# Two weights of a slot converted as one 1024-column tile, splits between the layers on VectorE, and the second block three slots behind the first

## The chip, the cores and the metric

The kernel runs on one core of a Trainium2 chip. The metric is the device time of one execution in microseconds (us). Before the change three runs gave 947.40, 947.91 and 949.22 us, with a median of 947.91 us.

## The reference, cut to what matters

Four sequences of 576 tokens go through windowed attention with eight heads of 64 columns (heads 0 to 3 look back 32 positions, heads 4 to 7 look back 128 positions in steps of four). The result, 2304 tokens by 512 columns, goes through two MLPs of 2048 hidden columns; the first has a leaky ReLU, the second a softplus.

```python
scores = np.where(masks, scale * q @ k.T, -1e9)        # per batch and head
attn = np.exp(scores - scores.max(-1)); attn /= attn.sum(-1) + 1e-9
x = concat_heads(attn @ v)                             # 2304 x 512
h = x @ w_in;  x = np.maximum(0.01 * h, h) @ w_out     # first layer
h = x @ w_in2; out = softplus(h) @ w_out2              # second layer
```

The weights arrive as 64-bit floats, q, k and v as 32-bit floats. On the chip each weight is turned from two 32-bit words into one 32-bit float, and that float is split into a high part in TensorE's fast format (fp32r) and a low part, the rest. Every product of an MLP is three matmuls: high by high, high by low, low by high.

## The kernel before, in words

**Slots.** The hidden columns of a layer are cut into 16 groups f of 128. A slot is one group f for one block of tokens. It has a first product (12 matmuls, `first_product`, L622, tile h) and, two slots later on TensorE (LAG = 2), a second product (12 matmuls, `g2`, L665, tile yp). Between them ScalarE applies the leaky ReLU (`g1_leaky`, L638, tile hc) and rounds to the high part (`g1_hi`, L643, gh), and VectorE subtracts to get the low part (`g1_lo`, L647, gl). There are two banks for h, two tiles hc, three gh and three gl. The second layer has the same shape (h in L622, softplus in L718 to L738, gh L744, gl L748, second product yo in L761).

**Blocks.** The first layer goes over eight blocks of tokens: 256, 256, 352 and five of 288. The list `order` sets the slots. Block 0 runs LEAD = 6 slots alone, then blocks 1 and 0 alternate, (1,0), (0,6), (1,1), (0,7) and so on, until both have all 16 groups; the later blocks run one after the other.

**Conversion of a weight.** A piece is one weight (w_in or w_out) of one group f, 512 columns wide. Its raw words are loaded on SyncE's DMA queue (L224, L228, tile raw, 512 KB). ScalarE does rebias (L234, tile cf) and low (L248), VectorE shift (L239, tile cp), join (L243) and add (L252). In the first layer ScalarE then writes the high part (`split_hi`, L272) and VectorE the low part (`split_lo`, L277) into the weight tile w. The pieces of the second layer are converted during the first layer and stored to DRAM (L261); in the last 16 slots of the first layer each is loaded again into the place of a used weight (`reload`, L266), split by ScalarE (L272) and by GpSimd (L277 on POOL). The reload of w_in waits for the last first product that reads its place, that of w_out for the last second product.

**Attention.** A pair is two heads on a window of 288 tokens; there are 8 windows w of 4 pairs. Windows 0 and 1 are early: k and q rows are loaded (L389), transposed by TensorE (L431, tile tr), and the scores (L480, L484, tile sc) are copied out, one half by ScalarE and one by VectorE (`scores_copy`, L498 and L500). GpSimd takes the maximum (`rowmax`, L535), VectorE subtracts it (L539), ScalarE takes the exponent (L542), TensorE multiplies with v (`pv`, L555), VectorE normalises (L565 to L567, tile xn), TensorE transposes back (`xT`, L575), and x is split (x_hi L596, x_lo L600). Block 0 needs window 0, block 1 also window 1, block 2 also window 2. The early tiles lie where weights of groups 6 to 15 come later.

**Order.** Nothing is ordered by hand. Every operation is an `Op` with an engine, a cost, what it depends on, buffers that it takes and gives back, and a target time; `run_schedule` plays the program with these costs and picks on each engine the ready Op with the earliest due time. The list that comes out is the program order on every engine, and an engine that meets an instruction whose data isn't there waits, with all that is queued behind it.

Of the kernel before, what the change touches and what calls it, by code (L numbers as in the profile page):

```python
# [22 lines left out]
def kernel(  # L23
# [62 lines left out]
    class Op:  # L86
        def __init__(self, eng, cost, fn, *args, deps=(), order=(), acq=(), rel=(),
                     target=None, margin=0.0, start=0.0, lib=None):
# [6 lines left out]
            self.lib = lib  # L95
# [3 lines left out]
    def run_schedule(slots):  # L99
# [13 lines left out]
        def lag(a, b):  # L113
            if b.eng == "bw":
                return 2.0
            return late.get(a.eng, LATS if a.eng == b.eng else LAT)
# [9 lines left out]
        for o in reversed(order):  # L126
# [4 lines left out]
            o.prio = o.raw - o.margin  # L131
# [21 lines left out]
        now = 0.0  # L153
        finish = []
        while True:
# [7 lines left out]
            for e in engines:  # L163
# [3 lines left out]
                for o in pools[e]:  # L167
                    if ready_at[o] <= now + 1e-9 and all(free[a] >= o.acq.count(a) for a in o.acq):
                        rank = o.prio + (HOLD if switch(o) else 0.0), o.n
# [8 lines left out]
                if e == "dve" and lib[0] == "standard":  # L178

                    best.end += 0.5 * min(best.cost, max(0.0, busy["pool"] - now))  # L180
# [29 lines left out]
    NRAW, NCV = 2, 3  # L210

    class Piece:
        def __init__(self, layer, f, which):
            self.layer, self.f, self.which = layer, f, which

        def load(self):
            src = wsrc[self.layer][self.which]
            f = self.f
            if self.layer == 0:
                raw = wpool.tile([P, 2 * DM], U32, tag=f"w{self.which}_{f}", name="raw")  # L220
            else:
                raw = wraw.tile([P, 2 * DM], U32, tag="raw", name="raw", bufs=NRAW)
            if self.which == 0:
# [5 lines left out]
            self.raw = raw.rearrange("p (n t) -> p n t", t=2)  # L229

        def rebias(self):
            self.cf = wraw.tile([P, DM], U32, tag="cf", name="cf", bufs=NCV)
# [4 lines left out]
        def shift(self):  # L237
            self.cp = wraw.tile([P, DM], U32, tag="cp", name="cp", bufs=1)
            nc.vector.tensor_single_scalar(  # L239
                out=self.cp, in_=self.cf, scalar=3, op=ALU.logical_shift_left)  # L240
# [10 lines left out]
        def add(self, eng):  # L251
            eng.tensor_tensor(out=self.cf, in0=self.cf, in1=self.raw[:, :, 0], op=ALU.add)  # L252

        def new_part(self):
            self.w = wpool.tile([P, 2, DM], F32R, tag=f"w{self.which}_{self.f}", name=f"w{self.which}")
            wparts[self.layer, self.f, self.which] = self.w
# [6 lines left out]
        def reload(self):  # L263
            self.new_part()
            self.cff = self.w[:, 1].bitcast(F32)
            nc.sync.dma_start(out=self.cff, in_=w2_d[self.f, self.which])  # L266

        def split_hi(self, eng):
            if self.layer == 0:
                self.new_part()  # L270
            if eng is nc.scalar:
                nc.scalar.activation(out=self.w[:, 0], in_=self.cff, func=AF.Copy)  # L272
            else:
                eng.tensor_copy(out=self.w[:, 0], in_=self.cff)

        def split_lo(self, eng):
            eng.tensor_sub(out=self.w[:, 1], in0=self.cff, in1=self.w[:, 0].bitcast(F32))  # L277
# [10 lines left out]
    NQB, NKB, NVB = 2, 2, 3  # L288
# [8 lines left out]
    early_kq = [wpool.tile([P, KT + T1], F32, tag=f"w0_{NF - NE + i}", name="ekq") for i in range(NE)]  # L297
    early_s = [wpool.tile([P, 2 * T1], F32, tag=t, name="es")
               for t in [f"w1_{NF - NE + i}" for i in range(NE)] + [f"w0_{NF - 2 * NE + i}" for i in range(NE)]]
    early_v = [wpool.tile([P, 2, DIL, D + 1], F32, tag=f"w1_{NF - 2 * NE + i}", name="ev") for i in range(NE)]  # L300
    early_mx = [wpool.tile([P, 2 * T1], F32, tag=f"w{i}_{NB}", name="emx") for i in range(2)]
# [49 lines left out]
    class Pair:  # L351
# [25 lines left out]
        def load_rows(self, which, eng):  # L377
# [5 lines left out]
            if self.dil:  # L383
                t = wpool.tile(shape, F32, tag=f"w{which}_{NB - 1}", name="rows")
# [110 lines left out]
        def scores_copy(self, j):  # L495
            o = self.s[:, :, j]
            if j == 0:
# [108 lines left out]
    LEAD = 6  # L606
# [175 lines left out]
    SWITCH, HOLD = 6.8, 14.0  # L782
    SLOT1, SLOT2 = 3.75, 4.2
    MA, MC, MC1, MG, MY = 9.0, 4.0, 6.0, 3.0, 5.0
# [3 lines left out]
    COLD = 1.6  # L788
    TL, TR = 30.0, -12.0
# [336 lines left out]
```

## Time and profile before

| what | value |
| --- | --- |
| median of three runs | 947.91 us |
| profiled execution, its own time | 949.02 us |
| its span, first to last instruction | 947.2 us |
| TensorE (PE) busy | 924.1 us, 98% |
| VectorE (DVE) busy | 662.5 us, 70% |
| ScalarE (ACT) busy | 465.7 us, 49% |
| GpSimd (POOL) busy | 117.5 us, 12% |
| mean granted TensorE clock | 0.995 |

A profile comes from one execution. Ends of matmuls are modelled and overlap, so that busy TensorE isn't TensorE at its peak; the distance from the start of one group of matmuls to the start of the next is the better measure. In the tables of stretches the clock is the granted share of full speed. In a timeline, the words in brackets behind a row are the idle time of the engine before it and what ended that.

### The profile page before, as it was taken

What the parts mean: (1) busy time and instruction counts of PE and PEld (TensorE: products, weight loads), DVE (VectorE), ACT (ScalarE), POOL (GpSimd) and SP (SyncE); (2) the same over time, 40 slices, a digit from 0 to 9 for tenths busy, and PEclk for the clock granted to TensorE, in tenths of its full rate; (3) what the DMA queues carried; (4) which work ended last, traced back from release to release, by engine and by line L of the source; (5) the groups of instructions that cost most, each with busy time, mean ns of one, the idle gap of its engine ahead of it and who ended that gap; (6) DMA issues with size and microseconds to landing.
All of it is one profiled execution on the core that took longest, in us unless ns stands there. A gap on an engine that the chain in (4) does not pass through costs nothing.

```text
span 947.2 us, 15869 instructions
## 1 busy us (share of the span) xinstructions
PE 924.1 (98%) x6005; PEld 873.1 (92%) x6006; DVE 662.5 (70%) x1324; ACT 465.7 (49%) x975; POOL 117.5 (12%) x82
## 2 busy tenths in 40 slices
PE   7989989999999999999999999999999999999998
PEld 6789989999999999999999889899899899999996
DVE  6699996276574674756635787877877877877775
ACT  5578753334434344444456554644644645544544
POOL 4300001020020110101127810000000000000000
PEclk9999989999999999999999999999999999999999
DMA  9839114344454453643258400200200000000000
GB/s 220 254 75 371 20 33 72 101 109 107 127 133 121 108 142 99 147 129 101 76 179 266 151 21 1 66 1 1 67 1 1 34 1 1 34 1 1 34 0 35
DMA packets 139905, 81.52 MB, mean 86 GB/s; under 512 B 101172, under 2 KB 124724, under 8 KB 139828
## 3 DMA queue, kind: packets, MB, share of 16 engines
q1 hardware_dynamic: 137428, 79.92, 29.9%
q10 hardware_dynamic: 2400, 0.59, 0.3%
q8 instruction: 47, 0.77, 0.3%
q14 instruction: 30, 0.25, 0.1%
HBM read 62.65 MB, written 17.83 MB: 85 GB/s over the span
## 4 chain that ended last, share of the span: by engine, by line
PE 84%; DVE 5%; DMA 2%; issue 1%; ACT 1%; SPq 0%; POOL 0%; DVEq 0%; POOLq 0%; ACTq 0%
PE h L622 39%; PE yo L761 21%; PE yp L665 19%; PE sc L511 2%; PE pv L555 2%; DMA w<-w 1%; DMA yr<-y 1%; PE xt L575 1%; DVE cf L252 1%; DVE w L277 1%; DVE cf L243 1%; DMA raw<-in_moe_w_in_dram 0%; DVE gl L647 0%; DVE cp L239 0%; DMA y<-ys 0%
## 5 line engine op out<-in xcount | busy, mean ns | idle before, releaser
L622 PE MATMUL h<-xh,w 128*128 128x384 f32 (+3 forms) x1792 | 443.3, 317 | 0.2 <-ACT hc L638 0.2
L622 PEld LDWEIGHTS h<-xh,w 128*128 128x128 f32 x1792 | 313.9, 189 | 4.9 <-ACT hc L638 0.7
L622 PE MATMUL h<-xl,w 128*128 128x384 f32 (+3 forms) x896 | 281.6, 314 | 0.0
L665 PE MATMUL yp<-gh,w 128*128 128x288 f32 (+2 forms) x1024 | 231.3, 301 | 0.0
L761 PE MATMUL yo<-w,gh 128*128 128x512 f32 x576 | 180.5, 394 | 1.5 <-ACT gh L744 1.3
L622 PEld LDWEIGHTS h<-xl,w 128*128 128x128 f32 x896 | 169.9, 190 | 4.5 <-DVE xl L600 0.2
L665 PEld LDWEIGHTS yp<-gh,w 128*128 128x128 f32 x1024 | 173.4, 190 | 0.0
L665 PE MATMUL yp<-gl,w 128*128 128x288 f32 (+2 forms) x512 | 152.3, 297 | 2.9 <-DVE gl L647 2.9
L718 ACT ACTIVATE hc<-h 128x384 f32<-128x384 f32 x96 | 47.1, 490 | 181.0 <-PE h L622 181.0
L638 ACT ACTIVATE hc<-h 128x288 f32<-128x288 f32 (+2 forms) x128 | 52.1, 407 | 157.6 <-PE h L622 153.4
L761 PEld LDWEIGHTS yo<-w,gh 128*128 128x128 f32 x576 | 106.8, 188 | 20.0 <-ACT gh L744 3.0
L647 DVE TENSOR_TENSOR gl<-hc,gh 128x288 fp32r<-128x288 f32 (+2 forms) x128 | 69.8, 548 | 73.0 <-ACT gh L643 72.4
L761 PE MATMUL yo<-w,gl 128*128 128x512 f32 x288 | 114.5, 398 | 0.0
L665 PEld LDWEIGHTS yp<-gl,w 128*128 128x128 f32 x512 | 97.4, 190 | 3.7 <-DVE gl L647 3.6
L535 POOL PARTITION_ALL_REDUCE mx<-s x24 | 49.0, 2044 | 357.0 <-DVE s L525 349.9
L729 DVE TENSOR_SCALAR z<-hc 128x384 f32<-128x384 f32 x96 | 35.7, 372 | 76.9 <-ACT hc L719 76.9
L761 PEld LDWEIGHTS yo<-w,gl 128*128 128x128 f32 x288 | 54.1, 188 | 13.6 <-DVE gl L748 1.2
L643 ACT ACTIVATE gh<-hc 128x288 fp32r<-128x288 f32 (+2 forms) x128 | 56.7, 443 | 3.0
L736 DVE TENSOR_TENSOR ln<-ln,hc 128x384 f32<-128x384 f32 x96 | 54.5, 568 | 3.2
L732 DVE TENSOR_TENSOR z<-hc,z 128x384 f32<-128x384 f32 x96 | 54.5, 568 | 3.0
L748 DVE TENSOR_TENSOR gl<-ln,gh 128x384 fp32r<-128x384 f32 x96 | 53.6, 558 | 3.5 <-ACT gh L744 1.4
L738 DVE SCALAR_TENSOR_TENSOR ln<-h,ln 128x384 f32<-128x384 f32 x96 | 53.5, 557 | 3.2
(73 smaller groups left out, 1023.5 us busy)
## 6 DMA issues: line engine op xcount, KB each, us to landing
raw<-in_moe_w_in_dram SPq DMA_DIRECT2D x32, 512.0 KB
raw<-in_moe_w_out_dram SPq DMA_DIRECT2D x32, 512.0 KB
w<-cf SPq DMA_DIRECT2D x32, 256.0 KB
w<-w SPq DMA_DIRECT2D x32, 256.0 KB
out_dram<-o SPq DMA_DIRECT2D x18, 256.0 KB
qr<-in_q_dram SPq DMA_DIRECT2D x96, 36.0 KB
y<-ys SPq DMA_DIRECT2D x20, 144.0 KB
v<-in_v_dram SPq DMA_DIRECT2D x30, 64.0 KB
```

Of the source, the lines that this page charges most:

```text
L535: nc.gpsimd.partition_all_reduce(self.mx, self.sf, channels=P, reduce_op=bass_isa.ReduceOp.max)
L622: nc.tensor.matmul(out=h, lhsT=a[:, c, :], rhs=b_[:, c, :], start=(c == 0 and a is whi and b_ is xh), stop=(c == NC - 1 and a is wlo))
L638: nc.scalar.activation(out=hc, in_=hbank.pop(s), func=AF.Prelu, alpha=0.01)
L643: nc.scalar.activation(out=gh, in_=hcopy[s], func=AF.Copy)
L647: eng.tensor_sub(out=gl, in0=hcopy.pop(s), in1=gparts[s][0].bitcast(F32))
L665: nc.tensor.matmul(out=ybank[e][:, o:o + n], lhsT=a[:, e * P:(e + 1) * P], rhs=b_, start=(f == 0 and n == unit_len[u] and a is whi and b_ ...
L718: nc.scalar.activation(out=ex, in_=hbank[NS1 + s], func=AF.Abs)
L732: nc.vector.tensor_sub(out=z, in0=ex, in1=z)
L736: nc.vector.tensor_tensor(out=ln, in0=ln, in1=ex, op=ALU.min)
L738: nc.vector.scalar_tensor_tensor(out=ln, in0=hbank.pop(NS1 + s), scalar=0.0, in1=ln, op0=ALU.max, op1=ALU.add)
L748: nc.vector.tensor_sub(out=gl, in0=soft.pop(s)[1], in1=gparts[NS1 + s][0].bitcast(F32))
L761: nc.tensor.matmul(out=obank[c, t], lhsT=a[:, t * P:(t + 1) * P], rhs=b_, start=(f == 0 and a is gh and b_ is whi), stop=(f == NF - 1 and ...
```

## The change

- A piece of the first layer is now one group f with both weights: two loads into one raw tile, then every step of the conversion once, over 1024 columns (the add counts 2048, in halves of words). The weight tile holds both weights of a group. Pieces of the second layer stay at 512 columns. There are two cf tiles instead of three.
- The early tiles are parts of shared tiles (`borrow`).
- Both halves of the early scores are copied by ScalarE (NCOPY = 2).
- LEAD is 3 instead of 6.
- The second layer's `split_lo` after the reload runs on VectorE, and both reloads of a group wait for its last second product, since they share a tile.
- Two v buffers instead of three for the later windows.
- The planner has other costs for attention's matmuls, an added slack ahead of them, a term for VectorE operations within 1.2 us of a maximum on GpSimd, and other margins.

```diff
-    NRAW, NCV = 2, 3
+    NRAW, NCV = 2, 2
-            self.cf = wraw.tile([P, DM], U32, tag="cf", name="cf", bufs=NCV)
+            self.cf = wraw.tile([P, self.n], U32, tag="cf", name="cf", bufs=NCV)
...
         def split_hi(self):
             if self.layer == 0:
                 self.new_part()
+                self.hi, self.lo = self.w[:, :, 0], self.w[:, :, 1]
+                self.cff = self.cff.rearrange("p (w n) -> p w n", w=2)
+            nc.scalar.activation(out=self.hi, in_=self.cff, func=AF.Copy)
+        def split_lo(self):
+            nc.vector.tensor_sub(out=self.lo, in0=self.cff, in1=self.hi.bitcast(F32))
...
-    NQB, NKB, NVB = 2, 2, 3
+    NQB, NKB, NVB = 2, 2, 2
+    def borrow(f, which, n):
+        if f not in lent:
+            lent[f] = wpool.tile([P, 4 * DM], F32, tag=f"w{f}", name="lent")
+        return lent[f][:, 2 * DM * which:2 * DM * which + n]
...
-            if j == 0:
+            if j < NCOPY:
                 nc.scalar.activation(out=o, in_=self.sc[j], func=AF.Copy)
...
-    LEAD = 6
+    LEAD = 3
...
+                if best.lib == "reduce":
+                    locked = now + LOCK
+                if best.lock and now < locked:
+                    best.end = locked + best.cost
...
-    pieces = [(0, f, which) for f in range(NF) for which in (0, 1)]
+    pieces = [(0, f, None) for f in range(NF)] + [(1, f, which) for f in range(NF) for which in (0, 1)]
...
-            o = Op("dma", 0.5, a.reload, deps=[w2_stored[f, which], (g2_of if which else g1_of)[s]], **m)
-            o = Op("act", act(512), a.split_hi, nc.scalar, deps=[o], **m)
-            wready[1, f, which] = Op("pool", 1.45, a.split_lo, nc.gpsimd, deps=[o], lib="standard", **m)
+            o = Op("dma", 0.5, a.reload, deps=[w2_stored[f, which], g2_of[s]], **m)
+            o = Op("act", act(512), a.split_hi, deps=[o], **m)
+            wready[1, f, which] = Op("dve", dve(512), a.split_lo, deps=[o], **m)
```

What this does to the order is shown at three places. On VectorE, where blocks 0 and 1 alternate, a round before converts half a group and makes one gl (the first row is the split's low part of one piece):

```order
L277 TENSOR_TENSOR w_1071<-cf,w_1071 128x512
L252 ISA cf<-raw,cf 128x1024
L239 TENSOR_SCALAR cp<-cf 128x512
L647 TENSOR_TENSOR gl<-hc,gh 128x256
L243 SCALAR_TENSOR_TENSOR cf<-cf,cp 128x512
```

A round after converts a whole group and makes two gl:

```order
L298 TENSOR_TENSOR w<-cf,w 128x2x512
L676 TENSOR_TENSOR gl<-hc,gh 128x256
L268 ISA cf<-raw,cf 128x2048
L255 TENSOR_SCALAR cp<-cf 128x1024
L676 TENSOR_TENSOR gl<-hc,gh 128x256
L259 SCALAR_TENSOR_TENSOR cf<-cf,cp 128x1024
```

The four conversion rows stand once per group instead of twice; the gl rows keep their number and size.

On SyncE's queue at the start of the program, the k rows of window 1 (80x4x64) stood behind five loads of weights:

```order
L224 DMA raw_163<-in_moe_w_in_dram 128x4x256
L228 DMA raw_166<-in_moe_w_out_dram 128x1024
L224 DMA raw_169<-in_moe_w_in_dram 128x4x256
L228 DMA raw_176<-in_moe_w_out_dram 128x1024
L224 DMA raw_184<-in_moe_w_in_dram 128x4x256
L389 DMA rows_192<-in_k_dram 80x4x64 x4
L389 DMA rows_221<-in_q_dram 96x4x64 x3
```

After the change they stand behind six, two for each of three raw tiles:

```order
L239 DMA raw_152<-in_moe_w_in_dram 128x4x256
L243 DMA raw_152<-in_moe_w_out_dram 128x1024
L239 DMA raw_157<-in_moe_w_in_dram 128x4x256
L243 DMA raw_157<-in_moe_w_out_dram 128x1024
L239 DMA raw_166<-in_moe_w_in_dram 128x4x256
L243 DMA raw_166<-in_moe_w_out_dram 128x1024
L418 DMA rows_181<-in_k_dram 80x4x64 x4
L418 DMA rows_209<-in_q_dram 96x4x64 x3
```

The other load of the third group has moved ahead of the rows.

On VectorE at the end of the first layer (gl belongs to a slot of the first layer, xl<-yr to the first tokens of the second), only these two kinds stood there before:

```order
L647 TENSOR_TENSOR gl_6310<-hc_6288,gh_6305 128x288
L647 TENSOR_TENSOR gl_6335<-hc_6328,gh_6332 128x288
L647 TENSOR_TENSOR gl_6380<-hc_6373,gh_6375 128x288
L705 TENSOR_TENSOR xl_6416<-yr_6357,xh_6415 128x384 x2
L647 TENSOR_TENSOR gl_6441<-hc_6418,gh_6422 128x288
L705 TENSOR_TENSOR xl_6416<-yr_6357,xh_6415 128x384 x2
L647 TENSOR_TENSOR gl_6487<-hc_6463,gh_6470 128x288
L647 TENSOR_TENSOR gl_6532<-hc_6506,gh_6511 128x288
```

After the change the low parts of the reloaded weights stand between them (w_6145 is group 3, w_6208 group 4, w_6252 group 5):

```order
L676 TENSOR_TENSOR gl_6178<-hc_6165,gh_6173 128x288
L298 TENSOR_TENSOR w_6145<-w_6145 128x512 x2
L676 TENSOR_TENSOR gl_6218<-hc_6210,gh_6213 128x288
L734 TENSOR_TENSOR xl_6234<-yr_6175,xh_6233 128x384
L298 TENSOR_TENSOR w_6208<-w_6208 128x512
L734 TENSOR_TENSOR xl_6234<-yr_6175,xh_6233 128x384 x2
L676 TENSOR_TENSOR gl_6278<-hc_6254,gh_6272 128x288
L734 TENSOR_TENSOR xl_6234<-yr_6175,xh_6233 128x384
L298 TENSOR_TENSOR w_6208<-w_6208 128x512
L298 TENSOR_TENSOR w_6252<-w_6252 128x512 x2
L676 TENSOR_TENSOR gl_6321<-hc_6300,gh_6317 128x288
```

Each gl of the last slots now stands behind splits that wait for a reload and for ScalarE.

## Rows read from the trace of the kernel before

**Rows 1.** Busy time by stretch (us), with counts, granted clock and DMA share.

```profile
core 0: us, PE busy (x) PEld busy (x) DVE busy (x) ACT busy (x) POOL busy (x), PEclk, DMA share, GB/s
47.80:75.60 27.80, 23.77 (x181) 23.02 (x180) 26.34 (x60) 19.76 (x43) 2.26 (x1) 0.94 0.45 127
75.60:114.00 38.40, 38.39 (x328) 38.19 (x329) 37.01 (x76) 33.66 (x70) 0.00 (x0) 1.00 0.54 187
123.20:148.00 24.80, 21.54 (x159) 20.73 (x158) 22.52 (x45) 10.63 (x23) 4.43 (x2) 0.86 0.22 40
494.00:534.00 40.00, 36.88 (x269) 35.73 (x268) 24.68 (x23) 24.35 (x55) 30.66 (x23) 1.00 0.72 231
534.00:552.00 18.00, 16.85 (x95) 15.03 (x94) 16.30 (x22) 11.84 (x25) 11.43 (x8) 1.00 0.31 92
```

**Rows 2.** Timeline of TensorE (start us, length us): slots 0, 1 and 6.

```profile
47.87 0.56 PE L622 MATMUL h<-xh,w 128*128 128x256 f32 x1
...
52.92 0.63 PE L622 MATMUL h<-xh,w 128*128 128x256 f32 x2
...
53.51 0.39 PE L622 MATMUL h<-xh,w 128*128 128x256 f32 x2
...
75.63 0.37 PE L622 MATMUL h<-xh,w 128*128 128x256 f32 x1
```

**Rows 3.** TensorE's waits, 47.8 to 165.2 us: total, times, longest.

```profile
PE xt L575 <- DVE xn L567: 4.0, 3, 2.5
```

**Rows 4.** Timeline of VectorE where blocks 0 and 1 alternate.

```profile
80.12 0.42 DVE L239 TENSOR_SCALAR cp<-cf 128x512 uint32<-128x512 uint32 x1
80.46 0.41 DVE L647 TENSOR_TENSOR gl<-hc,gh 128x256 fp32r<-128x256 f32 x1
80.79 0.68 DVE L243 SCALAR_TENSOR_TENSOR cf<-cf,cp 128x512 uint32<-128x512 uint32 x1
...
82.04 0.68 DVE L252 CUSTOM_DVE_ANT_0 cf<-raw,cf 128x1024 uint16<-128x1024 uint16 x1
82.64 0.42 DVE L239 TENSOR_SCALAR cp<-cf 128x512 uint32<-128x512 uint32 x1
```

**Rows 5.** The chain that ended last: start, length, what; two products.

```profile
78.95 1.40 PE h L622 x12
...
470.93 1.60 PE yp L665 x12
```

**Rows 6.** The chain around 136 us.

```profile
136.81 2.62 PE yp L665 x12
```

**Rows 7.** TensorE's longest waits, 500 to 560 us.

```profile
PE yp L665 <- DVE gl L647: 2.9, 3, 1.6
PE yo L761 <- ACT gh L744: 1.0, 1, 1.0
```

**Rows 8.** Groups by line, mostly 500 to 552 us; behind |: busy us, mean ns.

```profile
L647 DVE TENSOR_TENSOR gl<-hc,gh 128x288 fp32r<-128x288 f32 x12 | 14.9, 1260 | 10.4 <-ACT gh L643 10.4
...
L272 ACT ACTIVATE w<-w 128x512 fp32r<-128x512 f32 x24 | 14.7, 624 | 8.6 <-DMA w<-w 8.5
...
L277 POOL TENSOR_TENSOR w<-w 128x512 fp32r<-128x512 f32 x32 | 45.5, 1453 | 40.2 <-ACT w L272 35.8 <-PE yp L665 2.4 <-DMA y<-ys 2.0
```

**Rows 9.** Start: the DMA issue of k rows, a stretch's DMA, TensorE's transposes.

```profile
9.22 3.13 SPq L389 DMA_DIRECT2D rows<-in_k_dram  x4
...
12.00:13.00 1.00, 1.00 (x12) 0.86 (x9) 1.00 (x1) 0.52 (x1) 1.00 (x1) 1.00 1.13 400
...
19.57 2.29 PE L431 MATMUL tr<-ident,rows 80*128 80x80 f32 x14
```

**Rows 10.** The chain, 494 to 513 us: transfers on it.

```profile
494.96 2.65 DMA w<-w
...
500.75 6.50 DMA yr<-y
...
512.48 4.81 DMA w<-w
```

More of the change, by code (lines that the diff above doesn't have):

```diff
@@ L152, in run_schedule @@
         result = []
-        now = 0.0
+        now = locked = 0.0
+        opened = False
         finish = []
@@ L177, in run_schedule @@
                 best.start, best.end = now, now + best.cost + switch(best)
-                if e == "dve" and lib[0] == "standard":
-                    best.end += 0.5 * min(best.cost, max(0.0, busy["pool"] - now))
+                if best.lib == "reduce":
+                    locked = now + LOCK
+                if best.lock and now < locked:
+                    best.end = locked + best.cost
+                if best.fn is g1:
+                    opened = True
+                if best.optional and opened:
+                    best.end, best.skip = now, True
                 if best.lib:
@@ L249, in low, with add @@
                 out=self.raw[:, :, 0], in_=self.raw[:, :, 0], func=AF.Copy, scale=2.0 ** -29)
-        def add(self, eng):
-            eng.tensor_tensor(out=self.cf, in0=self.cf, in1=self.raw[:, :, 0], op=ALU.add)
+        def add(self):
+            nc.vector.tensor_tensor(out=self.cf, in0=self.cf, in1=self.raw[:, :, 0], op=ALU.add)
         def new_part(self):
-            self.w = wpool.tile([P, 2, DM], F32R, tag=f"w{self.which}_{self.f}", name=f"w{self.which}")
-            wparts[self.layer, self.f, self.which] = self.w
+            if (self.layer, self.f) not in wroom:
+                wroom[self.layer, self.f] = w = wpool.tile([P, 2, 2, DM], F32R, tag=f"w{self.f}", name="w")
+                for i in range(2):
+                    wparts[self.layer, self.f, i] = w[:, i]
+            self.w = wroom[self.layer, self.f]
+            if self.layer:
+                self.w = self.w[:, self.which]
         def store(self):
@@ L383, in load_rows @@
             if self.dil:
-                t = wpool.tile(shape, F32, tag=f"w{which}_{NB - 1}", name="rows")
+                t = borrow(NB - 1, which, nb * 4 * D)[0:n // nb].rearrange("p (i h d) -> p i h d", i=nb, h=4)
             else:
@@ L935 @@
     prev_load = None
-    pieces = [(0, f, which) for f in range(NF) for which in (0, 1)]
-    pieces += [(1, f, which) for f in range(NF) for which in (0, 1)]
+    pieces = [(0, f, None) for f in range(NF)] + [(1, f, which) for f in range(NF) for which in (0, 1)]
     w2_stored = {}
-    early = [r for w, r in reduces if w < 2]
     for layer, f, which in pieces:
@@ L956 @@
[L956 to L976 removed]
+        landed = []
@@ new lines @@
+        for i in (0, 1) if which is None else (which,):
+            prev_load = Op("dma", 0.5, a.load, i, deps=free_w, order=[prev_load], acq=["raw"] if layer else [], start=es, **m)
+            landed.append(Op("bw", 1.75, lambda: None, deps=[prev_load], **m))
+        n = DM if layer else 2 * DM
+        o = Op("act", act(n), a.rebias, deps=landed, acq=["cf"], **m)
+        lw = Op("act", act(n), a.low, order=[o], **m)
+        o = Op("dve", dve2(n), a.shift, deps=[o], acq=["cp"], lock=True, **m)
@@ L977 @@
+        o = Op("dve", dve(n), a.join, deps=[o], rel=["cp"], lock=True, **m)
+        o = Op("dve", dve(n), a.add, deps=[o, lw], rel=["raw"] if layer else [], lock=True, **m)
+        if layer == 0:
+            o = Op("act", act(n), a.split_hi, deps=[o], **m)
+            wready[0, f] = Op("dve", dve(n), a.split_lo, deps=[o], rel=["cf"], lock=True, **m)
+        else:
+            w2_stored[f, which] = Op("dma", 0.5, a.store, deps=[o], rel=["cf"], target=c2, **m)
             last_conv.append(w2_stored[f, which])
-    for w, r in reduces:
-        if w >= 2:
-            r.order += pool_w1
```

144 lines of the change are left out of this document (61 added, 83 removed).

## The prediction, as put on record

> **What bounds the kernel now.** I read the table of busy times first: TensorE is busy for 98% of the span, so only three things can move the time: its idle time, stretches in which its matmuls run at half pace, and its work, which this change leaves alone (every group of 12 matmuls is there before and after). I then read the stretches one after another for idle time [rows 1]. Behind the first 48 us, three places hold nearly all of it.
>
> The first is the start of the first layer. Between slot 0 and slot 6 [rows 2] TensorE is idle for 27.80 − 23.77 = 4.0 us and VectorE is busy for 26.3 of 27.8 us [rows 1]. VectorE converts groups 0 to 5 there and finishes window 1's attention; TensorE's waits name it (xt waits for xn, 4.0 us in all) [rows 3]. The first matmuls there also run at half pace: two take 0.63 us at 52.92 and 0.39 us at 53.51 [rows 2], which is the 1.2 GHz level against the 2.4 GHz level, although the granted clock of the stretch reads 0.94 [rows 1].
>
> The second is the pinch. From 75.6 to 114 us TensorE has no idle time, but VectorE is busy for 37.0 of 38.4 us [rows 1]: both are close to the bound. One round on VectorE, half a group and a gl, takes 82.64 − 80.12 = 2.52 us [rows 4], so 5.04 us for a group, in which TensorE does four products of 1.40 us [rows 5], 5.60 us. That is 90%, and from 123 to 148 us, where window 2's attention comes on top, VectorE falls behind: TensorE is idle for 24.80 − 21.54 = 3.26 us and the granted clock is 0.86, with one product taking 2.62 us [rows 1, 6].
>
> The third is the seam of the layers. From 494 to 552 us TensorE is idle for 3.12 + 1.15 us [rows 1], and waits for gl and for the first gh of the second layer [rows 7]. In this stretch a gl takes 1.26 us on average, beside GpSimd's splits of 1.45 us each [rows 8]; a gl of about this size takes 0.41 us at 80.46 [rows 4]. From 552 us to the end the change touches nothing.
>
> **The change part by part.** *Start.* Slot 6 before begins at 75.63, with 6 first and 4 second products done, so 54 of the 64 groups of blocks 0 and 1 remain. After the change the same interleaving begins at slot 3, with 3 and 1 done and 60 left. Six more groups at 1.40 us are 8.4 us: slot 3 must begin before 75.63 − 8.4 = 67.2 us, or the earlier start gains nothing. When does it begin? Slot 0 began at 47.87. The k rows of window 1 now stand behind one more load of 512 KB: at 400 GB/s that is 1.3 us, and one more issue is up to 0.8 (four took 3.13 us); I take 1.9 us for both, and no slack hides it, since the transposes of these rows, at 19.57 before [rows 9], stand earlier in TensorE's order now. One more pv stands ahead of slot 0; of the attention's 7.0 us worked out next I take 2.0 for it. That makes 51.8. Up to slot 3 TensorE has four products (5.6 us) and a part of what window 1's attention left it: 23.77 busy less ten products (14.0) less half pace from 47.87 to 53.5 (about 2.7) is 7.0 us; I take 3.1 of it for the two pv and three xT that stand there. Sum 8.7 us at full pace, so 60.5; all at half pace about 15.8, so 67.6. With as much half pace as before (+2.7) and waits of 1.3, 64.5. Gain 67.2 − 64.5 = 2.7, taken as 2.5; ends: 67.6 + 2.0 of waits, a loss of 2.4, and 60.5, a gain of 6.7.
>
> *Pinch.* Eight instructions of 512 columns for a group become four of 1024, so 64 fewer over 16 groups. A 256-column gl holds VectorE for 0.33 us (80.46 to 80.79), the add and the joins and splits about 0.60 (82.04 to 82.64) [rows 4]: 1.05 ns a column and 0.06 us for each instruction. So 4 x 0.06 = 0.24 us saved per group, 3.8 us in all, and VectorE needs 4.80 of 5.60 us, 86%. The larger effect is when a weight is due: the first product of group f stands in slot 2f − 3 instead of 2f − 6, three slots or 8.4 us of TensorE later. Both work on the same loss: 3.26 us idle, plus between 1.2 us (one product of 2.62 instead of 1.40) and 3.5 us (14% of 24.8) at the low level. The ends are 0 and 6.8; I take 4.0, since window 2's attention still falls among the last conversions. The eight copies of scores that leave VectorE lie before slot 0, where TensorE is the bound; on ScalarE (33.7 of 38.4 us busy even from 75.6 to 114 [rows 1]) they have the same cover. If that is gone, eight copies of about 0.4 us (the nearest row is the gl of 0.41 [rows 4]) lose at most 3; I take nothing.
>
> The Trainium skill bears on this term: "VectorE: DVE Perf Modes", section "The TRN2 errata — SBUF-src ops pay a fixed extra latency per instruction", has a measured fixed term of about 150 cycles at 0.96 GHz, 0.156 us, for each VectorE instruction, and says that tiles of 512 elements and more spread it enough, which speaks against merging pieces that already had 512. Rows 4 show 0.06 us between starts, since the rest overlaps. By the page's figure 64 instructions fewer would give VectorE 10 us and the pinch would go whole, 6.8 instead of 4.0: an estimate of 937 us, inside the forecast's own range.
>
> *Seam.* GpSimd's splits go, and with them the slow gl. That frees up to the 3.1 us of idle time in 494 to 534. What comes in: 32 splits of 0.60 us on VectorE, in its queue ahead of a gl. The high and low parts of reload f stand before the work of slot f + 4, and the reload is issued after the second product of f. TensorE then has six products of 1.60 [rows 5] until slot f + 6 needs that h bank: 9.6 us, less 1.5 for two splits of 0.62 on ScalarE [rows 8] and the activation, 8.1 us for the transfer. A reload landed in 2.65 us, and in 4.81 behind a yr load, which itself took 6.50 [rows 10]. So most land in time. Behind the wait stand leaky, hi and gl of the slot; were one late, TensorE would stop two products later. The upper bound is a reload that waits for a whole yr load: 6.50 + 2.65 to 6.50 + 4.81 = 9.2 to 11.3 us, 1.1 to 3.2 us too late, at four loads 4.3 to 12.8 us. At the seam's end two splits now stand inside the first softplus chain, +1.2 us (up to 3.5 with a late transfer) on a chain for which TensorE already waits 1.0 us [rows 7]. Value: 3.1 − 1.6 = 1.5 gain; ends a gain of 4.3 and a loss of 12.8 + 1.6 − 3.1 = 11.3.
>
> *The rest.* Two v tiles instead of three: the v load of a pair waits for the pv two pairs earlier; outside the three places TensorE hardly waits, and the pairs of the later windows lie several slots apart, which hides a load; a late v would cost about one transfer, 2.7 us [rows 10]. I take nothing. Two cf tiles of 1024 hold more than three of 512: nothing.
>
> Sum: 2.5 + 4.0 + 1.5 = 8.0 us. The profiled execution took 949.02 us (span 947.2), 1.1 above the median of 947.91. So 941.0 on its own scale, and 940 against the median.
>
> **The rivals.** *B, most of it stays.* Slot 3 begins at 67 or later, VectorE is still the bound up to the end of the conversions and has only its 3.8 us less, of which TensorE gets part: 944 to 948. For it: VectorE is over 94% busy from 47.8 to 114 [rows 1], and an earlier start of TensorE gives it no time. Against: up to slot 3 it has three groups fewer to convert than up to slot 6.
>
> *C, all three in full.* 6.7 + 6.8 + 4.3 = 17.8 us: 930 against the median, 930 to 935 with a us or two left over. For it: the idle time is really there. Against: all three terms would be at their ends.
>
> *D, slower by late reloads.* The queue on SyncE is in order, and each of four yr loads stands just ahead of a reload for which ScalarE and VectorE now stop with the slot's own work behind. With three and more us lost at each, the seam costs 11.3 instead of gaining 1.5: 949.0 − 6.5 + 11.3 = 953.8, or 952.7 against the median. It decides from four overruns of 2.5 us, that is reloads landing 10.6 us after their product. Against: a yr load is issued one slot (3.2 us) before that reload and has half its 6.50 us behind it, so 4.81 is the nearer row.
>
> **How the numbers follow.** As forecast (936 to 944) 0.50; B 0.20; C 0.16; D, or a start and a seam that both lose, 0.14. A measurement can tell about 0.2% here, 1.9 us, so faster is below 946.0: the forecast, C and half of B, 0.50 + 0.16 + 0.10 = 0.76; B's other half, 0.10, is the same; D is slower, 0.14. Range 931 to 948, which leaves out D and the tip of C.
>
> **What would show it.** Start: slot 3 begins between 61 and 67 us; later than 67 refutes the term. Pinch: TensorE's idle time beside window 2's attention falls below 1.5 us, its granted clock stays above 0.95, and block 2 (the first product of 352 tokens) begins some 6.5 us earlier than before. VectorE's round for a group with two gl takes about 4.8 us. Seam: gl between 494 and 534 falls to about 0.45 us, waits of yp for gl vanish, and waits of ScalarE's w for the reload stay below 8 us from their product. A reload landing later than that, or TensorE waiting for h behind the activation, would show D. If TensorE's idle time falls and the time doesn't, a longer product in the chain (half pace) would be the reason.

## The result, and the profile after

Four runs of the changed kernel gave 939.00 to 941.81 us, median 940.79; the kernel before had 948.57 us over its four (947.40 to 949.56). The ratio is 0.9916, 95% interval 0.9896 to 0.9937. A second measurement on another chip gave 941.14 against 949.89 us, ratio 0.9907 (0.9889 to 0.9925). The profiled execution after is the fastest of its four, 939.00 us with a span of 937.2, so the two traces lie 10.0 us apart where the medians lie 7.8 and 8.8. The second measurement left a second profile of the same kernel (942.35 us, span 940.6), 6.6 us from the one before; it is the run "after again" below.

Busy time by stretch after the change, on the columns of [rows 1]: ahead of slot 0, slot 0 to slot 3, the alternating blocks, the pinch, then the seam's two parts.

```profile
8.75:55.20 46.45, 42.61 (x283) 36.37 (x284) 29.64 (x55) 26.16 (x54) 21.24 (x20) 1.00 0.86 224
55.20:66.70 11.50, 10.49 (x95) 10.05 (x96) 10.35 (x27) 8.38 (x16) 0.00 (x0) 1.00 0.68 205
66.70:114.00 47.30, 46.82 (x400) 46.62 (x399) 45.63 (x63) 37.87 (x60) 1.40 (x1) 1.00 0.54 177
114.00:148.00 34.00, 32.51 (x289) 32.30 (x289) 32.11 (x56) 20.44 (x35) 9.50 (x4) 1.00 0.18 34
488.00:526.00 38.00, 38.00 (x285) 38.00 (x285) 26.45 (x48) 27.33 (x59) 0.00 (x0) 1.00 0.81 263
526.00:545.00 19.00, 18.64 (x103) 16.71 (x102) 15.51 (x33) 13.01 (x27) 0.00 (x0) 1.00 0.38 115
```

At the seam TensorE is idle for 0.36 us instead of 4.27. In the pinch it is idle for 1.49 us instead of 3.26, and the granted clock stays at 1.00. Slot 0 to slot 3 takes 11.5 us. The first row is the surprise: it ends at 55.20, and slot 0 was expected at 51.8.

TensorE's timeline after (as [rows 2]): slot 0, slot 3, block 2, the second layer.

```profile
55.22 0.56 PE L651 MATMUL h<-xh,w 128*128 128x256 f32 x1
...
66.73 0.37 PE L651 MATMUL h<-xh,w 128*128 128x256 f32 x1
...
160.13 0.32 PE L651 MATMUL h<-xh,w 128*128 128x352 f32 x1
...
525.02 0.34 PE L651 MATMUL h<-xh,w 128*128 128x384 f32 x1
```

The last two of them in the kernel before:

```profile
165.22 0.32 PE L622 MATMUL h<-xh,w 128*128 128x352 f32 x1
...
534.40 0.34 PE L622 MATMUL h<-xh,w 128*128 128x384 f32 x1
```

So the two profiled executions part by 5.09 us up to block 2, by another 4.29 us (369.18 against 364.89) up to the second layer, and by 0.62 us from there to the end. In the second profile of the kernel after, slot 3 stands here:

```profile
67.72 0.36 PE L651 MATMUL h<-xh,w 128*128 128x256 f32 x1
```

Block 2 begins at 161.53 there and the second layer at 528.29, so the same three differences are 3.69, 2.42 and 0.49 us. Between these two executions of one kernel the starts move by 0.2 us at slot 0, 1.0 at slot 3, 1.4 at block 2 and 3.3 at the second layer, so a difference of that size between two profiles says little by itself.

VectorE's round after (as [rows 4]):

```profile
75.77 1.22 DVE L268 CUSTOM_DVE_ANT_0 cf<-raw,cf 128x2048 uint16<-128x2048 uint16 x1
76.90 0.69 DVE L255 TENSOR_SCALAR cp<-cf 128x1024 uint32<-128x1024 uint32 x1
77.50 0.97 DVE L495 STREAM_TRANSPOSE qz<-qr 64x288 f32<-64x288 f32 x2
78.50 0.43 DVE L676 TENSOR_TENSOR gl<-hc,gh 128x256 fp32r<-128x256 f32 x1
78.84 1.22 DVE L259 SCALAR_TENSOR_TENSOR cf<-cf,cp 128x1024 uint32<-128x1024 uint32 x1
80.01 0.43 DVE L676 TENSOR_TENSOR gl<-hc,gh 128x256 fp32r<-128x256 f32 x1
80.35 1.22 DVE L298 TENSOR_TENSOR w<-cf,w 128x1024 fp32r<-128x1024 f32 x1
81.49 1.22 DVE L268 CUSTOM_DVE_ANT_0 cf<-raw,cf 128x2048 uint16<-128x2048 uint16 x1
```

From add to add is 5.72 us; 1.00 of it are two transposes of attention, so a whole group with two gl takes 4.72 us (forecast 4.80, before 5.04).

The seam after: VectorE's gl and splits by line (as [rows 8]).

```profile
L298 DVE TENSOR_TENSOR w<-w 128x512 fp32r<-128x512 f32 x32 | 21.5, 689 | 11.4 <-ACT w L295 11.0
L676 DVE TENSOR_TENSOR gl<-hc,gh 128x288 fp32r<-128x288 f32 x12 | 5.5, 456 | 0.4
```

The same stretch by waits of all engines (as [rows 7]).

```profile
ACT w L295 <- DMA w<-w: 10.9, 10, 2.3
...
PE yo L790 <- DVE gl L777: 0.3, 1, 0.3
```

A gl takes 456 ns instead of 1260. ScalarE waits for a reload 2.3 us at most, and TensorE has 0.3 us of waits left.

And GpSimd at the start after the change, behind the first memsets:

```profile
8.61 0.28 POOL masks.py:199 TENSOR_SCALAR_AFFINE_SELECT ident<-ident 128x128 f32<-128x128 f32 x1 [7.67 <-issue]
...
19.57 0.38 POOL L355 PARTITION_ALL_REDUCE warm<-ident  x1 [9.45 <-issue]
```

Before, the first of these started at 1.22 us and the second at 9.17, behind a single gap of 6.44 us:

```profile
1.22 0.29 POOL masks.py:199 TENSOR_SCALAR_AFFINE_SELECT ident<-ident 128x128 f32<-128x128 f32 x1 [0.29 <-POOL ident masks.py:197]
...
9.17 0.38 POOL L326 PARTITION_ALL_REDUCE warm<-ident  x1 [6.44 <-issue]
```

TensorE's first transpose needs ident and so began at 8.95, where the kernel before began at 3.63. The prediction had no price for that.

### The profile page after: what moved, and what is told of

The parts are those of the page before. It is cut to its first block, busy times and chain, and to the rows that moved or that the text cites. A ratio compares the mean times of both kernels' runs of the same rounds, so it can differ in the third digit from the quotient of the medians.

```text
span 937.2 us, 15722 instructions
## 1 busy us (share of the span) xinstructions
PE 916.5 (98%) x6005; PEld 868.0 (93%) x6006; DVE 648.5 (69%) x1284; ACT 462.8 (49%) x935; POOL 72.4 (8%) x49
## 4 chain that ended last, share of the span: by engine, by line
PE 91%; DVE 5%; issue 1%; ACT 1%; DMA 1%; POOL 0%; SPq 0%; POOLq 0%; DVEq 0%; ACTq 0%
PE h L651 41%; PE yo L790 21%; PE yp L694 20%; PE pv L584 4%; PE sc L540 2%; PE sc L513 1%; PE tr L460 1%; PE xt L604 1%; DVE w L298 1%; DVE cf L259 1%; DMA raw<-in_moe_w_out_dram 1%; DVE gl L676 0%; PE sc L509 0%; DVE xl L629 0%; DVE cf L268 0%
## 5 line engine op out<-in xcount | busy, mean ns | idle before, releaser
L694 PE MATMUL yp<-gh,w 128*128 128x288 f32 (+2 forms) x1024 | 228.7, 299 | 0.0
L694 PEld LDWEIGHTS yp<-gh,w 128*128 128x128 f32 x1024 | 171.5, 188 | 0.0
L676 DVE TENSOR_TENSOR gl<-hc,gh 128x288 fp32r<-128x288 f32 (+2 forms) x128 | 60.7, 475 | 53.5 <-ACT gh L672 52.7
```

The lines of the kernel that those rows point to most:

```text
L676: eng.tensor_sub(out=gl, in0=hcopy.pop(s), in1=gparts[s][0].bitcast(F32))
L694: nc.tensor.matmul(out=ybank[e][:, o:o + n], lhsT=a[:, e * P:(e + 1) * P], rhs=b_, start=(f == 0 and n == unit_len[u] and a is whi and b_ ...
```

## The experiments

All times below are medians, and the ratio is to the kernel before on the same chip. Starts are those of one profiled execution each (us), and move as said above; ratios carry an interval of about ±0.002, so differences of two of them below that are read with the trace or not at all.

| run | slot 0 | block 2 | second layer | median | ratio (95%) |
| --- | --- | --- | --- | --- | --- |
| before | 47.87 | 165.22 | 534.40 | 948.57 | 1 |
| after | 55.22 | 160.13 | 525.02 | 940.79 | 0.9916 (0.9896–0.9937) |
| subtraction at the end | 54.57 | 160.45 | 526.78 | 940.65 | 0.9908 (0.9890–0.9927) |
| one library | 53.42 | 159.49 | 523.64 | 939.82 | 0.9897 (0.9877–0.9917) |
| before, splits on VectorE | 51.70 | 169.73 | 536.66 | 950.56 | 1.0010 (0.9995–1.0025) |
| same, subtraction at the end | 47.79 | 163.14 | 529.59 | 946.74 | 0.9970 (0.9955–0.9985) |
| one library, rows behind four loads | 52.27 | 158.40 | 525.68 | 938.73 | 0.9875 (0.9854–0.9896) |
| one library, LEAD 6 | 47.36 | 164.67 | 529.00 | 942.55 | 0.9921 (0.9901–0.9940) |
| one library, halves | 54.79 | 162.13 | 527.64 | 942.15 | 0.9918 (0.9896–0.9940) |
| before, LEAD 3 | 50.23 | 162.23 | 529.86 | 946.03 | 0.9956 (0.9937–0.9974) |
| after again | 55.44 | 161.53 | 528.29 | 941.14 | 0.9907 (0.9889–0.9925) |
| one library, rows behind two loads | 53.33 | 158.40 | 524.30 | 938.06 | 0.9879 (0.9860–0.9898) |
| after, splits on GpSimd | 54.74 | 160.13 | 527.81 | 946.03 | 0.9965 (0.9950–0.9979) |
| one library, NCOPY 1 | 53.51 | 164.14 | 530.20 | 942.01 | 0.9919 (0.9898–0.9940) |

**Which library GpSimd has left.** Theory 1 said that the kernel after starts each execution with the wrong GpSimd code, since its last GpSimd work is now a maximum; theory 2 that the late slot 0 is only the new order. Four runs: a subtraction put behind the last maximum,

```diff
             if not o.skip:
                 o.fn(*o.args)
+            if o is reduces[-1][1]:
+                nc.gpsimd.tensor_sub(out=masks[:, 0], in0=masks[:, 1], in1=masks[:, 1])
```

> The kernel after, with one GpSimd subtraction of 96 columns behind the last row maximum (a result that nobody reads), which brings GpSimd's other code library back before the program ends. Theory 1 (library): the late slot 0 of the kernel after (55.22 us against 47.87) comes from GpSimd, which has to load the library of the masks first (7.67 us of issue) and then that of the maxima (9.45 us), because the last GpSimd work of the program is now a maximum. Then here the first mask operation starts at about 1.2 us instead of 8.61, the warm-up maximum at about 9 instead of 19.57, slot 0 at 48 to 52, slot 3 at 60 to 63 instead of 66.73, and the median is 935 to 938. Theory 2 (order): slot 0 is late because window 1's rows and one more pv stand ahead of it, and GpSimd's load is hidden. Then slot 0 stays at 54 to 56 and the median within 2 us of 940.8.

a warm-up maximum ahead of the masks,

```diff
     def setup():
+        t = attp.tile([P, 1], F32, tag="warm", name="warm")
+        nc.gpsimd.memset(t, 0.0)
+        nc.gpsimd.partition_all_reduce(t, t, channels=P, reduce_op=bass_isa.ReduceOp.max)
         make_identity(nc, ident)
```

(the later warm-up is left out),

> The kernel after, with the warm-up maximum ahead of the masks instead of behind them, so that all of GpSimd's work in the program uses the library of the maxima and none is ever changed. Theory 1: no load longer than 1 us at the start (the library is still there from the execution before), first mask operation before 2 us, first maximum by about 12 us, median 934 to 938, equal to the run with the subtraction or up to 2 us better since the second load of 6 to 9 us goes too. Theory 2: as the kernel after, 939 to 943.

and in the kernel before the one edit that takes the other library off GpSimd's end, without and with the subtraction:

```diff
-            wready[1, f, which] = Op("pool", 1.45, a.split_lo, nc.gpsimd, deps=[o], lib="standard", **m)
+            wready[1, f, which] = Op("dve", dve(512), a.split_lo, nc.vector, deps=[o], **m)
```

> The kernel before with one edit: the low parts of the reloaded weights on VectorE instead of GpSimd, nothing else. Theory 1: GpSimd ends the program with a maximum, so the start loses what it lost in the kernel after: first mask operation at about 8.6 us, slot 0 some 4 to 7 us later than 47.87, and the seam gains 2 to 4 us; sum 948.6 + 3 = 949 to 953. Theory 2: the start is that of the kernel before, slot 0 at 48, and only the seam's gain is seen: 944 to 947.

> The same edit of the kernel before, with the GpSimd subtraction behind the last maximum. Both theories: slot 0 at 48 and the seam alone, 944.5 to 947 (gain 1.5 to 4 of the 4.3 us that TensorE is idle there before). Against the run without the subtraction, theory 1 says 4 to 7 us less, theory 2 no difference.

GpSimd's start with the subtraction at the end:

```profile
1.22 0.29 POOL masks.py:199 TENSOR_SCALAR_AFFINE_SELECT ident<-ident 128x128 f32<-128x128 f32 x1 [0.29 <-POOL ident masks.py:197]
...
10.14 0.38 POOL L355 PARTITION_ALL_REDUCE warm<-ident  x1 [7.42 <-issue]
```

With one library throughout:

```profile
0.97 0.36 POOL L335 PARTITION_ALL_REDUCE warm<-warm  x1
...
1.54 0.29 POOL masks.py:199 TENSOR_SCALAR_AFFINE_SELECT ident<-ident 128x128 f32<-128x128 f32 x1
```

In the kernel before with the splits on VectorE:

```profile
9.12 0.28 POOL masks.py:199 TENSOR_SCALAR_AFFINE_SELECT ident<-ident 128x128 f32<-128x128 f32 x1 [8.18 <-issue]
```

The mechanism of theory 1 is shown as far as the start goes: what GpSimd did last in a program decides how the same program starts the next time. With a maximum last there is a gap of 7.7 to 8.2 us ahead of the first mask; with an ordinary subtraction last the gap is 0.29 us; and with maxima first and last there is no gap at all. That the gap is a load of code is a reading of it: the trace has no row for a load and puts the gap down to "issue". One point stays open. In the run with one library the same masks start right behind a maximum without a gap, so they don't need the other code; why they wait in the kernel after, where a maximum was the last work of the execution before, the traces don't say. In the order of before it costs 3.8 us on one chip (950.56 against 946.74; slot 0 moves by 3.91), and it ate the whole gain of the seam, 3.5 us.

In the order of after theory 1's size failed: slot 0 moved only from 55.22 to 54.57 with the subtraction (48 to 52 expected) and to 53.42 with one library, and the medians of 940.65 and 939.82 can't be told from 940.79. With the loads gone TensorE meets another wait at once, in the run with the subtraction:

```profile
18.92 2.39 PE L460 MATMUL tr<-ident,rows 80*128 80x80 f32 x8 [1.78 <-DMA rows<-in_k_dram]
```

These are the k rows of window 1 behind six loads. The late library had hidden the late rows: TensorE began the first scores 3.3 us earlier (8.77 instead of 12.09) and gave back 1.78 here and 0.8 in slower transposes. So theory 2 was right on what comes last.

**The rows.** The two issues of window 1 go ahead of the third group's loads (and in the other run also ahead of the second's).

```diff
+    moved = [o for o in schedule if name(o) == "load_rows" and o.fn.__self__.w == 1][:2]
+    before_ = [o for o in schedule if name(o) == "load"][4]
+    schedule = [o for o in schedule if o not in moved]
+    i = schedule.index(before_)
+    schedule[i:i] = moved
```

> The kernel with one GpSimd library, and in SyncE's queue the k and q rows of window 1 behind four loads of weights instead of six. Theory 1 (rows): with the library's wait gone, TensorE stands 1.78 us for these k rows at 18.9 us and transposes them as they arrive (2.39 us instead of 1.57), and up to slot 0 nearly all is one gapless run at half pace; so the rows are what is left of the 3.3 us that the library cost. Slot 0 moves from 53.4 to 50.5 to 51.5, the median from 939.8 to 937 to 938. Theory 2: what ends last ahead of slot 0 is VectorE or ScalarE, and slot 0 stays within 1 us, the median at 939 to 941.

> One GpSimd library, and the k and q rows of window 1 behind two loads of weights instead of four or six. If the rows were still on the path with four (slot 0 at 52.27, TensorE without a gap from 8.9 us on), slot 0 would move by another us; the trace with four shows no wait for rows any more, so theory: slot 0 within 0.5 us of 52.3 and the median within 1 us of the run with four (938.7). Rival: conversions of groups 1 and 2 start later and TensorE waits for their weights, 1 to 2 us slower.

Slot 0 moved by 1.15 us with four loads, not 2 to 3 and not less than 1, and TensorE has no gap from 8.9 us to the xn waits. The median fell to 938.73. With two loads ahead a wait for v (1.6 us) takes the place, which neither the theory nor the rival had named; slot 0 is back at 53.33, and the median of 938.06 can't be told from 938.73. These two are the fastest of all, some 2 us below the kernel with one library, about one interval, so that the gain itself isn't settled.

**Due time or count.** In the kernel with one library LEAD alone is set back, then VectorE's merged instructions alone are halved:

```diff
-    LEAD = 3
+    LEAD = 6
```

> The kernel with one GpSimd library and LEAD = 6 instead of 3: the pieces stay merged, but the weight of group f is due three slots earlier again. Theory 1 (due time): the gain of the first 165 us is that of LEAD, so TensorE waits for weights and xn again, block 2 begins 3 to 6 us later than 159.5, median 943 to 946. Theory 2 (count): the gain is the 64 VectorE instructions saved, block 2 stays within 1.5 us, median 939 to 941.5.

```diff
-            nc.vector.tensor_single_scalar(
-                out=self.cp, in_=self.cf, scalar=3, op=ALU.logical_shift_left)
+            for i in range(0, self.n, DM):
+                nc.vector.tensor_single_scalar(
+                    out=self.cp[:, i:i + DM], in_=self.cf[:, i:i + DM], scalar=3, op=ALU.logical_shift_left)
```

(join, add and split_lo likewise)

> The kernel with one GpSimd library, each VectorE step of a first-layer conversion as two instructions of 512 columns one behind the other instead of one of 1024, in the same order (64 more instructions, 0.06 us each by the row of before, 3.8 us of VectorE in all). Theory 1 (due time): three slots of room hide it, block 2 moves by less than 1.5 us, median 939 to 941.5. Theory 2 (count): VectorE is the bound up to the last conversion, block 2 begins 2.5 to 4 us later, median 942 to 944.

And in the kernel before LEAD alone is changed:

```diff
-    LEAD = 6
+    LEAD = 3
```

> The kernel before with LEAD = 3 instead of 6 and nothing else. Theory 1 (due time): block 2 begins 3 to 6 us earlier than before (165.2), the median is 3 to 6 us below the kernel before on the same chip. Theory 2 (count): VectorE has as much to convert as before and TensorE catches up with it, less than 1.5 us gained.

Each theory is right on a part. Theory 1's sizes came at block 2 for LEAD 6 (5.2 us later than with one library) and for LEAD 3 in the kernel before (3.0 us earlier than 165.22), theory 2's for the halves (2.6 us later, median 942.15). TensorE's waits show more.

LEAD acts at the start. In the kernel before, LEAD 6, TensorE's waits from 47.8 to 75.6 us are these:

```profile
PE pv L555 <- ACT es L542: 3.2, 2, 2.1
PE xt L575 <- DVE xn L567: 1.5, 2, 0.8
```

With merged pieces, one library and LEAD 6 slot 0 starts early, and from 46 to 165 us TensorE then waits:

```profile
PE h L652 <- DVE w L298: 4.5, 4, 1.4
PE pv L585 <- ACT lent L572: 3.6, 3, 1.4
```

The wait of pv for ScalarE's exponents (es before, lent after) is gone with LEAD 3, in the order of before as in that of after. The wait of h for weights is 2.5 us in two with LEAD 3.

LEAD alone does not empty the pinch. From 114 to 148 us, the kernel before and the same with LEAD 3:

```profile
114.00:148.00 34.00, 30.74 (x235) 29.93 (x234) 31.04 (x59) 17.23 (x36) 6.76 (x3) 0.90 0.22 39
...
114.00:148.00 34.00, 29.85 (x248) 29.00 (x247) 33.16 (x69) 21.51 (x44) 4.19 (x2) 0.95 0.17 31
```

and merged pieces, one library and LEAD 6:

```profile
114.00:148.00 34.00, 34.00 (x304) 33.98 (x302) 31.30 (x54) 19.70 (x34) 5.93 (x3) 1.00 0.20 35
```

TensorE is idle for 3.26, 4.15 and 0 us. But the third run has its waits earlier: from 48 to 114 us TensorE is idle for 9.2 us there, for 4.0 before and for 1.5 with LEAD 3 in the kernel before. With the whole change and one library it is 3.3 and then 1.49 in the pinch. The number of VectorE instructions is a part of that: the run with halves is idle for 1.24 us there and for 1.36 us from 148 to 165, against 1.49 and 0 with whole pieces, and of the 2.6 us by which its block 2 is later 1.4 are there at slot 0 (54.79 against 53.42). VectorE's busy time from 75 to 114 us shows why, with whole pieces and one library:

```profile
75.00:114.00 39.00, 39.00 (x332) 39.00 (x331) 37.16 (x50) 32.04 (x50) 2.07 (x1) 1.00 0.41 125
```

and with halves:

```profile
75.00:114.00 39.00, 39.00 (x334) 39.00 (x333) 38.88 (x81) 31.61 (x50) 0.69 (x1) 1.00 0.44 135
```

31 more instructions cost 1.72 us, 0.055 each, and leave VectorE 0.1 us of room in 39. What else takes the pinch's idle time away (conversions of a whole group at a time, the copies on ScalarE, the planner's costs) these runs don't separate. Nor do they settle whether LEAD needs the merged pieces: at block 2 it is worth 5.2 us with them and 3.0 without, by the ratios about 2 with them (0.9897 against 0.9921, intervals that overlap) and about 4 without (0.9956).

How far a start in one profile can be trusted shows in a pair. The kernel before with splits on VectorE and the subtraction has the same operations in the same order as the kernel before up to block 2. At 136 us, behind the same wait of 2.54 us for xn, TensorE's starts in the two are 0.08 us apart. From 136 to 140 us the granted clock is then 0.50 in the kernel before, and in the other it stays at 1.00:

```profile
114.00:148.00 34.00, 30.03 (x255) 29.09 (x255) 32.88 (x63) 17.24 (x37) 7.18 (x4) 1.00 0.24 43
```

Its block 2 begins at 163.14, 2.1 us ahead of 165.22. So 2.1 us of what the profiles show up to block 2 is the price of the low level in one execution. Counted from 163.14, LEAD 3 in the kernel before, whose own clock fell as well (0.95), gains 0.9 us and not 3.0.

**The seam and the copies.**

```diff
-            wready[1, f, which] = Op("dve", dve(512), a.split_lo, deps=[o], **m)
+            wready[1, f, which] = Op("pool", 1.45, a.split_lo, nc.gpsimd, deps=[o], lib="standard", **m)
```

(`split_lo` takes the engine as an argument again),

> The kernel after with the low parts of the reloaded weights on GpSimd again (which also brings the other library back before the end, so that its start is that of the run with the subtraction). Theory (seam): gl at the seam takes over 1 us again, TensorE waits for it 3 to 4 us in all between 488 and 545, and the median is 3 to 4 us above the run with the subtraction (940.7), 943.5 to 945. Rival: the reloads now wait for the second product in any case and the splits are no longer what is late, less than 1.5 us, 940 to 942.

```diff
-    NCOPY = 2
+    NCOPY = 1
```

> One GpSimd library and one half of the early scores copied by VectorE again (NCOPY = 1). Prediction's term: nothing, 939 to 941, since the copies lie before slot 0 where TensorE runs without a gap. Rival: VectorE's conversions of the first groups come later by eight copies of 0.4 us, 3 us, and slots 1 and 2 wait for them: 941.5 to 943.

> The kernel after, unchanged, on one chip with the three runs beside it. If the two library loads at the start cost what the trace shows at slot 0 (55.22 against 53.42 us without any load), it stands 1 to 2 us above the run with one library (939.8 on another chip) and 2 to 3 us above the run with two loads of weights ahead of the rows. If the loads are hidden, there is no difference that can be told to the former.

With the splits back on GpSimd the kernel loses 4.9 us (946.03 against 941.14 on one chip). The seam's gl:

```profile
L676 DVE TENSOR_TENSOR gl<-hc,gh 128x288 fp32r<-128x288 f32 x12 | 13.3, 1117 | 12.0 <-ACT gh L672 12.0
```

and TensorE's waits from 480 to 560 us:

```profile
PE yo L790 <- ACT gh L773: 1.9, 1, 1.9
PE yp L694 <- DVE gl L676: 1.4, 1, 1.4
PE yo L790 <- DVE gl L777: 0.7, 1, 0.7
PE yo L790 <- ACT ys L702: 0.7, 1, 0.7
```

The theory had the size, but gl is 1.4 us of it, not 3 to 4: more than half of these 4.7 us of waits stands at the second layer's first yo, not at the first layer's yp. The profiles say the same: the run begins its second layer no later than the kernel after beside it (527.81 against 528.29) and takes 2.9 us longer from there to the end. The kernel after measured again beside it has slot 0 at 55.44 and the same first gap, 8.14 us: the start is no accident of one execution. Against the run with one library it stands 0.0010 higher in the ratio; that is 1 us, and the intervals overlap, so what the library costs this kernel's median isn't settled; it is small.

With one copy on VectorE slot 0 did not move (53.51), but block 2 came 4.65 us later. The whole order of the start changes with that number, and TensorE then waits for es, for v and behind kr just ahead of and in the first slots; its granted clock from 60 to 75 us is 0.66, where it is 1.00 with both copies on ScalarE:

```profile
60.00:75.00 15.00, 13.41 (x84) 12.69 (x85) 12.06 (x28) 8.62 (x15) 0.59 (x1) 0.66 0.75 260
```

The median of 942.01 is of the rival's size, but its ratio can't be told from that of the run with one library (0.9919 and 0.9897), and TensorE's wait for weights is 0.6 us, so the rival's mechanism isn't what the trace shows. Whether there is a loss, and whether the copies or the order would make it, stays open.

## Why the prediction was right

It said 940.0 us (931 to 948), faster with a chance of 0.76; the two medians are 940.8 and 941.1, and both intervals of the ratio lie below 1. That two of the three places gained, the pinch and the seam, is shown. That the sum came so near is in part luck: its terms missed in both directions. The first profile of the kernel after gives 0.5, 4.6 and 4.9 us for start, pinch and seam, the second −0.5, 4.2 and 2.9, where 2.5, 4.0 and 1.5 were forecast.

*Start, 2.5 forecast, nothing that both profiles show.* Slot 3 began at 66.73 in one and 67.72 in the other, on either side of the break-even of 67.2. The step that failed is slot 0 at 51.8; it began at 55.2 and 55.4. The rows cost what they were priced at or a little more, once nothing else hides them (1.9 taken; 1.78 of waiting and 0.8 of slower transposes with the subtraction at the end). But the term "one more pv, 2.0 us" left out the waits around it: ahead of slot 0 TensorE is idle for 3.2 of the last 15 us, where it was 1.7 before. And the sum knew nothing of GpSimd's libraries. The text priced GpSimd's splits by what they slow down and by the queue they leave; it did not ask what else the last operation of an engine leaves behind. From slot 0 to slot 3, 12.7 us were forecast (64.5 − 51.8) and 11.5 and 12.3 came. Two steps on the way don't hold as written. The 4.0 us of xT's waits for xn were read as the start's, but [rows 3] reach to 165.2 us: 1.5 of them lie between slot 0 and slot 6, where the longest wait is that of pv for ScalarE's exponents (3.2 us, shown above), and 2.5 lie in the pinch. And "all at half pace about 15.8" has no working, since twice 8.7 is 17.4; it sets only an end of the range.

*Pinch, 4.0 forecast, 4.6 and 4.2 measured* (5.1 and 3.7 up to block 2, less the start). Idle time of 1.49 us and the granted clock of 1.00 are what was asked for, and the round is 4.72 us for 4.80; block 2 came 5.1 and 3.7 us earlier, not 6.5. The price of the low level, taken as 1.2 to 3.5 us, is 2.1 us in the pair of equal order. The step that failed is "the larger effect is when a weight is due": LEAD 3 alone leaves the pinch's idle time at 4.15 us and takes waits from the start instead. What part of the 4.0 belongs to which cause stays open.

*Seam, 1.5 forecast, 4.9 and 2.9 measured* (4.3 and 2.4 to the second layer, 0.6 and 0.5 behind it). The runs put it at 3.5 us (the splits moved in the kernel before, with the subtraction at the end, on one chip) and 4.9 us (moved back in the kernel after). The 3.1 us of idle time went as forecast. The step that failed is the charge of 1.6 us for two splits inside the first softplus chain: TensorE's wait for that chain fell from 1.0 to 0.3 us. The slow gl was only one victim of GpSimd's splits; VectorE's softplus operations beside them were others. One of them in the second layer's first slots, before the change:

```profile
L734 DVE TENSOR_TENSOR ln<-ln,z 128x384 f32<-128x384 f32 x3 | 3.0, 1006 | 0.1
```

after it:

```profile
L763 DVE TENSOR_TENSOR ln<-ln,z 128x384 f32<-128x384 f32 x3 | 1.6, 550 | 0.0
```

and with the splits on GpSimd again:

```profile
L763 DVE TENSOR_TENSOR ln<-ln,z 128x384 f32<-128x384 f32 x2 | 2.7, 1374 | 0.1
```

An operation of 0.55 us takes 1.0 to 1.4 us on average there, and the chain has three of the kind, which together lose more than the two splits of 0.60 that now stand inside it cost.

*Rival D* is refuted. ScalarE waits for a reload 2.3 us at most, but the 8.1 us allowed count from the end of the group's second product. By that count the latest one for which ScalarE waited is one of group 5, whose product ends at 499.58 and whose split starts at 506.64, 7.1 us later:

```profile
497.98 1.60 PE yp L694 x12
...
506.64 0.63 ACT L295 ACTIVATE w<-w 128x512 fp32r<-128x512 f32 x1 [0.79 <-DMA w<-w]
```

*Rival B* came true at the start alone, where slot 3 began at about 67, for a reason of its own. *C* came near at the seam alone.

*The Trainium skill on VectorE.* "VectorE: DVE Perf Modes" in the Trainium skill, section "The TRN2 errata — SBUF-src ops pay a fixed extra latency per instruction", gives a measured fixed term of about 150 cycles in the duration of one instruction, 0.156 us, and by the prediction's estimate from it the pinch would have gone whole. The traces agree on the duration: 0.68 us for 512 columns and 1.22 for 1024 leave 0.14 that doesn't grow with the columns. But the next instruction starts before the last one ends, and between starts this kernel's rows show 0.055 to 0.07 us, before, after and with halves. 1.5 us of the pinch stayed: the measurement decides.

## What to carry to other kernels

When an engine loses its last use of a code library, look at its first instruction as well as at the place of the edit: the end of one execution is the start of the next. A wait that goes at the start is worth only what the next late input leaves, so price the second-latest too. Where two parts of a change are meant for one loss, run each alone and look where the waits go: here the later due time took them from the start and left those of the pinch, and the rest of the change with the old due time only moved them ahead of it. And take a second profile of the same kernel before a term of one or two us is called right or wrong.

## What the runs showed of the hardware

What GpSimd did last in one execution sets how the next one starts: in eight profiles (before, after twice, and five variants) the first gap follows what the same program did last (0.29 us behind a subtraction in five, 7.7 to 8.2 us behind a maximum in three). The gaps read as loads last 5.9 to 9.5 us: 5.9 to 7.4 ahead of the first maximum where a subtraction was last, 7.7 to 8.2 ahead of the first mask, and 9.2 and 9.5 for the second gap of the kernel after. "GPSIMD Engine Reference" in the Trainium skill, section "2.1 Instruction dispatch", gives about 6 us for the first call to freshly loaded code, with no instruction in the profile that shows it. The traces agree that nothing shows, only idle time put down to "issue"; their shortest gaps (5.9 and 6.0 us) agree with the figure, and the others are longer. Right behind a maximum the masks (affine selects) ran without a gap, and in the runs with one library GpSimd has no gap of this kind at the start.

TensorE's granted clock needn't fall behind a given wait: behind the same 2.54 us without work, with the same order of operations before it, it fell to 0.50 in one execution and stayed at 1.00 in another, and that was 2.1 us at block 2.

VectorE's operations were slower beside GpSimd's subtractions of 1.45 us: a gl of 128x288 took 1.12 to 1.26 us on average beside it, and 0.46 us without.
